# Transposes of q, k and x moved from the PE to DMA, in a kernel whose instruction order is planned beforehand

## The chip, the cores and the metric

One core of a Trainium2 chip. The time is device microseconds (us) of one execution, the median of several runs; lower is better. A ratio is the mean time of one kernel's fast runs over the mean of the other's fast runs of the same rounds on the same chip, so it is not quite the ratio of the medians quoted next to it. The runs were made in several calls on different chips; where times from two calls are compared, the ratios to the kernel before are what counts. All runs were in the fast state but one of e8 and one of e17; their ratios leave it out.

The engines are called PE (matrix products), DVE, ACT and POOL (here exponentials, masks, casts and copies) and SP (issues the DMAs here). Operands lie in one memory of the core, SBUF. In this kernel the PE writes its results to another, PSUM, and DVE or ACT copies them from there: 24 copies of 0.55 us for the transposed q and k of batches 1 to 3. The granted clock is the share of its full speed at which the PE was allowed to run.

## The reference

Attention with a window of 128 keys and 4 sink keys, over 4 batches, 8 heads, 768 positions and head dimension 64, followed by a two-layer network with a sigmoid-type gate on the 3072 tokens:

```python
scores = scale * q @ k.T                       # per batch and head
keep = (key < 4) | ((0 <= pos_q - pos_k) & (pos_q - pos_k < 128))
a = softmax(where(keep, scores, -1e9)) ; attn = a @ v
x = attn.transpose(0, 2, 1, 3).reshape(3072, 512)
h = x @ w_in                                   # 512 x 2048
out = (h * sigmoid(1.702 * h)) @ w_out         # 2048 x 512
```

## The kernel before

Work is cut into 32 units of one head pair and 384 positions (`kk`), 16 load groups of two units (`m`), and 8 slabs of the network (`n`), each fed by four units. The prediction calls a unit a head pair. Nothing is ordered by hand: every operation is declared with an engine, a duration that the author believes, and its predecessors, and a small scheduler plays the machine once when the kernel is built. It then emits the instructions in the order in which they started in that play. **Each engine executes its own instructions in that fixed order**, and SP's queue of DMA issues is one of the "engines". A wrong duration therefore cannot make the result wrong, but it puts instructions in an order that the chip then has to wait through.

```python
class Plan:
    LAG = {"PE": 0.2, "SP": 1.6}           # what a follower on another engine waits beyond the duration
    def order(self, idle):
        ...                                # pick, engine by engine, what can start first
            free[eng] = start + o["dur"]
            end[n] = free[eng] + self.LAG.get(eng, 0.12)
        ...
        return sorted(out, key=lambda x: x[:2])
```

Loads go over SP, three DMAs of 128 KB for each of q, k and v of a group in batches 1 to 3. POOL casts them to fp16; POOL also applies most of the masks, in the same fixed order:

```python
dur = 1.25 if b == 0 else 1.75
load(f"Lq{m}", dur, ...) ; load(f"Lk{m}", dur, ...) ; load(f"Lv{m}", 1.8, ...)
...
op(f"Cq{m}", "POOL", ...) ; op(f"Ck{m}", "POOL", ...)      # casts
op(f"MZ{kk}_{t}", "POOL", 0.4, ...)                        # masks of unit kk
op(f"V{kk}", "PE", ..., after=masked + ...)                # attention times v, waits for the masks
```

The parts that the change replaces, for batches 1 to 3:

```python
def t_mm():                                    # q and k of one unit: 6 transposes into PSUM
    for t in range(2):
        for i in range(NB):
            nc.tensor.transpose(tp[:, t, i], qk[:, t, i], ident16)
op(f"T{kk}", "PE", 0.36, t_mm, ...) ; op(f"Tc{kk}", "DVE", 0.65, ...)      # and a copy to SBUF
...
def x_mm():                                    # x of one unit: 3 transposes into PSUM
    for i in range(NB):
        nc.tensor.transpose(xt[:, i], T[f"xn{kk}"][:, i], ident16)
op(f"X{kk}", "PE", 0.2, x_mm, ...) ; op(f"Xc{kk}", "DVE", 0.37, x_copy, ...)
```

The softmax here doesn't subtract the row's maximum and nothing guards it: scores larger than these inputs give would overflow.

Of the kernel before, what the change touches and what calls it, by code (L numbers as in the profile page):

```python
# [14 lines left out]
P = 128  # L15
D = 64
SLAB = 384
NB = SLAB // P
# [19 lines left out]
class Plan:  # L38
# [14 lines left out]
    def op(self, name, eng, dur, emit, after=(), opens=(), uses=(), rank=0.0, at=0.0, starts=()):  # L53


        assert name not in self.ops
        self.ops[name] = dict(
            name=name, eng=eng, dur=dur, emit=emit, after=list(after), starts=list(starts),
            opens=list(opens), rank=rank, at=at,
        )  # L60
        for t in set(uses) | {t for _, t in opens}:
            self.users.setdefault(t, set()).add(name)
# [74 lines left out]
def kernel(  # L137
# [11 lines left out]
    nc = tc.nc  # L149
    Bsz, H, S, Dh = q.shape  # L150
# [6 lines left out]
    NHP = H // 2  # L157
    NU = 2 * NHP
# [7 lines left out]

    slots = dict(
        ps=8,
        qk32=4, v32=4, w32=3, qk16=4, v65=6, qkT=8, AT0=2, AT1=2, xnat=2, th=3, gT=2, xT=4, osb=2,
    )  # L170
    const = ctx.enter_context(tc.tile_pool(name="const", bufs=1))
    sb = ctx.enter_context(tc.tile_pool(name="sb", bufs=1))
# [2 lines left out]
    T = {}  # L175

    def new(name, shape, dt=FP16):
        tag, i = plan.slot_of[name]
        pool = psp if tag == "ps" else sb
        T[name] = pool.tile(list(shape), dt, tag=f"{tag}{i}", bufs=1, name=name)  # L180
        return T[name]
# [3 lines left out]
    ident16 = const.tile([P, P], FP16, name="ident16")  # L185
# [8 lines left out]
    op = plan.op  # L194
# [61 lines left out]
    def add_casts(m: int, eq: str, ek: str, ev: str):  # L256
        b, g, hp = where(2 * m)
        dur = {"DVE": 0.56, "ACT": 0.83, "POOL": 0.85}

        def qk(t, eng):  # L260
            if t == 0:
                new(f"qk16_{m}", (P, 2, NB, 4, D))
            dst, src = T[f"qk16_{m}"][:, t], T[f"qk32_{m}"][:, t]
            if b == 0:
                ENG[eng](  # L265
                    dst.rearrange("p i h d -> p h i d"),
                    src.rearrange("p (h i d) -> p h i d", i=NB, d=D),
                )
            else:
                ENG[eng](dst.rearrange("p i h d -> p (i h d)"), src)  # L270

        op(f"Cq{m}", eq, dur[eq], lambda: qk(0, eq), after=[f"Lq{m}"],
           opens=[("qk16", f"qk16_{m}")], uses=[f"qk32_{m}"], rank=2 * m)
        op(f"Ck{m}", ek, dur[ek], lambda: qk(1, ek), after=[f"Lk{m}", f"Cq{m}"],
           uses=[f"qk16_{m}", f"qk32_{m}"], rank=2 * m)

        def cv():
            v65 = new(f"v65_{m}", (P, NB, 4, D1))
            nc.gpsimd.memset(v65[:, :, :, D:D1], 1.0)
            ENG[ev](v65[:, :, :, 0:D], T[f"v32_{m}"])  # L280

        op(f"Cv{m}", ev, dur[ev] + 0.1, cv, after=[f"Lv{m}"], opens=[("v65", f"v65_{m}")],
           uses=[f"v32_{m}"], rank=2 * m + 0.5)
        if g == 0:
            def sink(c):
                pool(
                    vs[c][32 * c : 32 * c + n_sink, H * b + 2 * hp : H * b + 2 * hp + 4],
                    T[f"v65_{m}"][0:n_sink, 0],
                )

            for c in range(3):
                op(f"K{m}_{c}", "POOL", 0.44, lambda c=c: sink(c), after=[f"Cv{m}"],
                   uses=[f"v65_{m}"], rank=2 * m + (0.6 if c == 0 else 5))


    def qkT(kk):
        return T[f"qkT{kk}"]

    def half(kk: int):
        m, j = divmod(kk, 2)  # L300
        return T[f"qk16_{m}"][:, :, :, 2 * j : 2 * j + 2]
# [5 lines left out]
    def add_attention(kk: int, at: float):  # L307
        b, g, hp = where(kk)
        m = kk // 2
# [1 line left out]
        r = kk  # L311
        at_ = f"AT{kk}"
        prev = kk - NHP if g else kk
        qts = [f"qkT{kk}"] + ([f"qkT{prev}"] if g else [])

        if early:

            def t_mm(t):
                qk = half(kk)
                if t == 0:  # L320
                    new(f"qkT{kk}", (P, 2, NB, P))
                tp = new(f"tp{kk}_{t}", (P, SLAB), FP32)
                for i in range(NB):
                    nc.tensor.matmul(  # L324
                        tp, qk[:, t, i], spread[:, i], start=(i == 0), stop=(i == NB - 1)
                    )

            def t_copy(t, eng):
                eng(qkT(kk)[:, t].rearrange("d i s -> d (i s)"), T[f"tp{kk}_{t}"])

            for t, eng in enumerate(("DVE", "ACT")):
                op(f"T{kk}_{t}", "PE", 0.5, lambda t=t: t_mm(t),
                   after=[f"C{'qk'[t]}{m}", "spread"] + ([f"SA{kk - 1}"] if kk else []), opens=[("ps", f"tp{kk}_{t}")] + ([] if t else [("qkT", f"qkT{kk}")]),
                   uses=[f"qk16_{m}"], rank=r)
                op(f"Tc{kk}_{t}", eng, (0.56, 0.48)[t],
                   lambda t=t, eng=eng: t_copy(t, ENG[eng]),
                   after=[f"T{kk}_{t}"] + ([f"Tc{kk}_0"] if t else []),
                   uses=[f"tp{kk}_{t}", f"qkT{kk}"], rank=r)
            ready = [f"Tc{kk}_0", f"Tc{kk}_1"]
        else:  # L340
            def t_mm():
                qk = half(kk)
                tp = new(f"tp{kk}", (P, 2, NB, P))
                for t in range(2):
                    for i in range(NB):
                        nc.tensor.transpose(tp[:, t, i], qk[:, t, i], ident16)  # L346

            op(f"T{kk}", "PE", 0.36, t_mm, after=[f"Cq{m}", f"Ck{m}", f"SA{kk - 1}"],
               opens=[("ps", f"tp{kk}"), ("qkT", f"qkT{kk}")], uses=[f"qk16_{m}"], rank=r, at=at)
            op(f"Tc{kk}", "DVE", 0.65,  # L350
               lambda: dve(new(f"qkT{kk}", (P, 2, NB, P)), T[f"tp{kk}"]),  # L351
               after=[f"T{kk}"], uses=[f"tp{kk}", f"qkT{kk}"], rank=r)
            ready = [f"Tc{kk}"]

        def mm(dst, h, key, i0, ni):
            nc.tensor.matmul(  # L356
# [10 lines left out]
        def s_z():  # L367
            Z = [new(f"Z{kk}_{h}", (P, 512), FP32) for h in range(2)]
            pk = qkT(prev)
            for h in range(2):  # L370
                mm(Z[h][:, 0:P], h, qkT(kk)[:, 1, 2], 2, 1)
            for h in range(2):
                if g:
                    mm(Z[h][:, P : 2 * P], h, pk[:, 1, 2], 0, 1)
                else:
                    mm(Z[h][:, P : 2 * P], h, pk[:, 1, 0], 2, 1)
            if g:
                for c in range(4):
                    for h in range(2):
                        mm(  # L380
                            Z[h][bass.ts(c, 32), 2 * P : 3 * P], h,
                            pk.rearrange("d t i s -> d t (i s)")[:, 1, 0:32], min(c, 2), 1,
                        )

        def e_a(h):
# [15 lines left out]
        op(f"SZ{kk}", "PE", (0.2, 0.36)[g], s_z, after=[f"SA{kk}"],  # L401
           opens=[("ps", f"Z{kk}_{h}") for h in range(2)], uses=qts, rank=r)
        for h in range(2):
            op(f"EA{kk}_{h}", "ACT", 0.5, lambda h=h: e_a(h),
               after=[f"SA{kk}"] + ([f"EA{kk}_0"] if h else []),
               opens=[] if h else [(f"AT{g}", at_)], uses=[f"A{kk}_{h}", at_], rank=r)
        for h in range(2):
            op(f"EZ{kk}_{h}", "ACT", (0.3, 0.4)[g], lambda h=h: e_z(h),
               after=[f"SZ{kk}", f"EA{kk}_1"], uses=[f"Z{kk}_{h}", at_], rank=r)

        def m_a():
# [13 lines left out]

        masked = []
        if g == 0 or early:
            op(f"MA{kk}", "DVE", 0.7, m_a, after=[f"EA{kk}_0", f"EA{kk}_1", "masks"], uses=[at_], rank=r)
            masked.append(f"MA{kk}")
        else:  # L430
            for t, sgn in ((0, 1), (1, -1)):
                op(f"MA{kk}_{t}", "POOL", 0.64,
                   lambda t=t, sgn=sgn: select(0, 8, 2, t, sgn), after=[f"EA{kk}_0", f"EA{kk}_1"],
                   uses=[at_], rank=r)
                masked.append(f"MA{kk}_{t}")
        for t, sgn in ((0, 1), (1, -1))[: 1 + g]:
            op(f"MZ{kk}_{t}", "POOL", 0.4,
               lambda t=t, sgn=sgn: select(8, 8 + 2 * SZ[g], SZ[g], t, sgn),
               after=[f"EZ{kk}_0", f"EZ{kk}_1"], uses=[at_], rank=r)
            masked.append(f"MZ{kk}_{t}")  # L440
# [47 lines left out]
        def x_copy():  # L488
# [1 line left out]
                new(f"xT{n}", (P, NHP, SLAB))  # L490
            dve(T[f"xT{n}"][:, hp].rearrange("p (i s) -> p i s", s=P), T[f"xt{kk}"])  # L491

        op(f"X{kk}", "PE", 0.2, x_mm, after=[f"N{kk}", "ident"], opens=[("ps", f"xt{kk}")],
           uses=[f"xn{kk}"], rank=r)
        op(f"Xc{kk}", "DVE", 0.37, x_copy, after=[f"X{kk}"] + ([f"Xc{kk - 1}"] if hp else []),
           opens=[] if hp else [("xT", f"xT{n}")], uses=[f"xt{kk}", f"xT{n}"], rank=r)


    def add_f(n: int, F: int):
# [17 lines left out]
        def f_mul():  # L517
# [8 lines left out]
           after=[f"Xc{4 * n + 3}", f"W{F // 4}"] + ([f"F{n}_{F - 1}"] if F else []),  # L526
           opens=[("ps", f"hT{nm}")] + ([] if F else [("gT", f"gT{n}")]),
           uses=[f"xT{n}"], rank=rank)
        op(f"H{nm}", "ACT", 0.42, f_tanh, after=[f"F{nm}"], opens=[("th", f"th{nm}")],
           uses=[f"hT{nm}"], rank=rank)  # L530
        op(f"G{nm}", "DVE", 0.555, f_mul, after=[f"H{nm}"],
           uses=[f"hT{nm}", f"th{nm}", f"gT{n}"], rank=rank)
# [150 lines left out]
```

## Time and profile before

| | before |
|---|---|
| time, median (three runs at first, a fourth with the change) | 249.29 us, 249.89 us |
| span of the profiled run | 247.7 us |
| PE busy | 231.7 us (94%) |
| PE without work between 50 and 160 us | 110.0 - 106.7 = 3.3 us |
| SP issues the last load of q, k or v until | 114.2 us |
| POOL's casts wait for loads of q, k and v | 13.7 us |

The stretch from 50 to 160 us, with the columns that the prediction explains, and the PE's wait for POOL's masks (us in total, times, longest):

```profile
50.00:160.00 110.00, 106.68 (x1080) 63.38 (x1081) 68.10 (x150) 64.83 (x149) 57.55 (x108) 1.00 0.65 144
...
PE av L461 <- POOL AT L420: 2.5, 3, 1.9
```

The PE is the engine to fill. Its busy time is that of overlapping matmul records, so what it says well is where the PE has nothing at all to do. POOL's waits matter only as far as they reach the PE.

### The profile page before, as it was taken

The page shows a single profiled execution, that of the slowest core. Times are in us where ns is not written, and L with a number is a line of the kernel's source. Part 1 is how long each engine was busy: PE and PEld are TensorE (multiplying, and loading weights), DVE is VectorE, ACT ScalarE, POOL GpSimd, SP SyncE. Part 2 cuts the span into 40 slices and gives each one's busy share as a digit, 9 for nine tenths or more (in the row PEclk, how much of TensorE's full clock was granted, in tenths as well). Part 3 has the DMA queues.
Part 4 walks back from the last instruction along what each step waited for, and adds up shares of the span by engine and source line. Part 5 has one row for each costly group of instructions (what it writes and reads, how often), then busy time and mean ns, then how long its engine had stood idle before and what let it go on. Part 6 is the DMA issues. An engine that isn't in the chain of part 4 may idle for free.

```text
span 247.7 us, 5387 instructions
## 1 busy us (share of the span) xinstructions
PE 231.7 (94%) x2065; PEld 132.8 (54%) x2065; DVE 135.8 (55%) x282; ACT 132.0 (53%) x291; POOL 102.1 (41%) x171
## 2 busy tenths in 40 slices
PE   0996999989999699999999999999999999999993
PEld 0453566556555465565555665556654554564441
DVE  6376589678646563378724787348731680382000
ACT  2472788367547472487644784458741661472111
POOL 7688487687467786643267400015330000000000
PEclk9998999999999999999999999999999999999999
DMA  7999999899997999996011100120002101201112
GB/s 186 294 371 282 329 356 315 199 230 216 237 242 184 231 202 237 225 241 146 3 45 42 45 3 0 51 79 4 0 10 77 42 3 44 83 0 45 75 53 86
DMA packets 75723, 34.14 MB, mean 138 GB/s; under 512 B 64177, under 2 KB 68657, under 8 KB 75697
## 3 DMA queue, kind: packets, MB, share of 16 engines
q1 hardware_dynamic: 75552, 33.76, 52.7%
q8 instruction: 16, 0.26, 0.5%
q14 instruction: 11, 0.08, 0.1%
q10 hardware_dynamic: 144, 0.03, 0.1%
HBM read 27.49 MB, written 6.29 MB: 136 GB/s over the span
## 4 chain that ended last, share of the span: by engine, by line
PE 72%; DMA 7%; POOL 7%; SPq 7%; ACT 2%; DVE 2%; issue 2%; ACTq 0%; POOLq 0%
PE o L542 30%; PE hT L507 25%; SPq L220 6%; DMA v<-in_v_dram 6%; PE av L461 4%; PE A L356 3%; PE tp L324 3%; PE tp L346 2%; POOL AT L420 2%; PE Z L356 2%; DMA qk<-in_k_dram 2%; PE xt L484 2%; DVE vs L587 1%; POOL w_in L253 1%; POOL v L280 1%
## 5 line engine op out<-in xcount | busy, mean ns | idle before, releaser
L507 PE MATMUL hT<-xT,w_in 128*128 128x384 f16 x512 | 92.6, 328 | 0.2 <-ACT AT L388 0.2
L542 PE MATMUL o<-w_out,gT 128*128 128x512 f16 x384 | 89.2, 379 | 0.0
L520 DVE SCALAR_TENSOR_TENSOR gT<-th,hT 128x384 f16<-128x384 f16 x128 | 67.1, 548 | 35.0 <-ACT th L513 31.6
L513 ACT ACTIVATE th<-hT 128x384 f16<-128x384 f32 x128 | 60.9, 504 | 30.1 <-PE hT L507 27.8
L507 PEld LDWEIGHTS <-w_in 128*128 128x128 f16 x512 | 47.6, 98 | 29.4 <-issue 1.4
L420 POOL TENSOR_SCALAR_AFFINE_SELECT AT<-AT 128x256 f16<-128x256 f16 (+1 forms) x72 | 35.1, 513 | 56.1 <-ACT AT L394 23.2
L542 PEld LDWEIGHTS <-gT 128*128 128x128 f16 x384 | 35.7, 98 | 38.1 <-issue 0.2
L388 ACT ACTIVATE AT<-A 128x512 f16<-128x512 f32 x64 | 34.7, 595 | 22.1 <-PE A L356 22.1
L560 ACT ACTIVATE osb<-o 128x512 f32<-128x512 f32 x23 | 13.8, 601 | 45.0 <-PE o L542 37.6
L394 ACT ACTIVATE AT<-Z 128x256 f16<-128x256 f32 (+1 forms) x64 | 24.8, 452 | 0.0
L270 POOL CAST qk<-qk 128x768 f16<-128x768 f32 x24 | 19.4, 824 | 9.4 <-PE tp L346 3.8
L461 PEld LDWEIGHTS <-AT 128*128 128x128 f16 x480 | 18.4, 97 | 8.9 <-POOL AT L420 3.7
L414 DVE TENSOR_TENSOR AT<-AT,masks 128x1024 f16<-128x1024 f16 x20 | 16.5, 824 | 12.0 <-ACT AT L388 11.9
L461 PE MATMUL av<-v,AT 128*128 128x65 f16 x352 | 19.2, 193 | 3.5 <-POOL AT L420 2.5
L470 DVE TENSOR_TENSOR xn<-av,rcp 128x384 f16<-128x384 f32 x32 | 17.8, 557 | 1.1
L356 PEld LDWEIGHTS <-qkT 64*128 64x128 f16 (+1 forms) x384 | 11.5, 93 | 11.9 <-DVE xT L491 3.0
L324 PE MATMUL tp<-spread,qk 128*128 128x384 f16 x48 | 11.5, 369 | 6.5 <-DVE qk L265 6.0
L351 DVE COPY qkT<-tp 128x768 f16<-128x768 f16 x24 | 13.2, 552 | 6.9 <-PE tp L346 6.8
L280 POOL CAST v<-v 128x768 f16<-128x768 f32 x16 | 13.2, 826 | 8.6 <-DMA v<-in_v_dram 8.4
L469 DVE RECIPROCAL rcp<-av 128x6 f32<-128x6 f32 x32 | 6.2, 194 | 17.9 <-PE av L461 17.4
L491 DVE COPY xT<-xt 128x384 f16<-128x384 f16 x32 | 11.3, 354 | 7.2 <-PE xt L484 5.9
L461 PE MATMUL av<-vs,AT 128*128 128x65 f16 x128 | 14.9, 193 | 0.0
(30 smaller groups left out, 131.4 us busy)
## 6 DMA issues: line engine op xcount, KB each, us to landing
v<-in_v_dram SPq DMA_DIRECT2D x48, 128.0 KB, 3.6
out_dram<-osb SPq DMA_DIRECT2D x23, 256.0 KB, 2.0
qk<-in_q_dram SPq DMA_DIRECT2D x36, 128.0 KB, 3.5
qk<-in_k_dram SPq DMA_DIRECT2D x36, 128.0 KB, 3.7
w<-in_moe_w_in_dram SPq DMA_DIRECT2D x4, 1024.0 KB, 7.1
w<-in_moe_w_out_dram SPq DMA_DIRECT2D x4, 1024.0 KB, 8.5
qk<-in_q_dram SPq DMA_DIRECT2D x4, 384.0 KB, 5.7
qk<-in_k_dram SPq DMA_DIRECT2D x4, 384.0 KB, 6.1
```

The source lines that it names most:

```text
L270: ENG[eng](dst.rearrange("p i h d -> p (i h d)"), src)
L324: nc.tensor.matmul(tp, qk[:, t, i], spread[:, i], start=(i == 0), stop=(i == NB - 1))
L356: nc.tensor.matmul(dst.rearrange("p (t s) -> p t s", s=P), key[hd[h]], qkT(kk)[hd[h], 0, i0 : i0 + ni], start=True, stop=True,)
L388: nc.scalar.activation(out=T[at_][:, 4 * h : 4 * h + 4].rearrange("p a s -> p (a s)"), in_=T[f"A{kk}_{h}"], func=AF.Exp, scale=scale,)
L394: nc.scalar.activation(out=T[at_][:, 8 + SZ[g] * h : 8 + SZ[g] * (h + 1)].rearrange("p a s -> p (a s)"), in_=T[f"Z{kk}_{h}"][:, 0 : SZ[g] ...
L420: nc.gpsimd.affine_select(out=ap, in_=ap, pattern=[[0, ap.shape[1]], [sgn, P]], compare_op=ALU.is_ge if sgn > 0 else ALU.is_gt, fill=0.0, ...
L461: nc.tensor.matmul(av[:, i, h], lhsT, rhs, start=(n == 0), stop=(n == len(terms) - 1))
L470: nc.vector.tensor_tensor(out=xn, in0=av[:, :, :, 0:D], in1=rcp.to_broadcast((P, NB, 2, D)), op=ALU.mult)
L507: nc.tensor.matmul(hT, w_in16[:, c, bass.ts(F, P)], T[f"xT{n}"][:, c], start=(c == 0), stop=(c == NHP - 1),)
L513: nc.scalar.activation(out=new(f"th{nm}", (P, SLAB)), in_=T[f"hT{nm}"], func=AF.Tanh, scale=0.851)
L520: nc.vector.scalar_tensor_tensor(out=T[f"gT{n}"][:, F], in0=T[f"th{nm}"], scalar=1.0, in1=T[f"hT{nm}"], op0=ALU.add, op1=ALU.mult,)
L542: nc.tensor.matmul(T[f"o{nm}"], T[f"gT{n}"][:, F, bass.ts(t, P)], w_out16[:, F], start=(F == 0), stop=(F == NF - 1),)
```

## The change

The intent is to take 216 transposes off the full PE, and their PSUM copies off DVE, and to let DMA do them from SBUF to SBUF: q and k of a group in one transpose of 384 KB, x of a unit in one of 96 KB. All are issued by SP, between the loads and the stores. Some durations of ACT, DVE and POOL are corrected on the way, and the numbers of buffers are changed.

```diff
-        qk32=4, v32=4, w32=3, qk16=4, v65=6, qkT=8, AT0=2, AT1=2, xnat=2, th=3, gT=2, xT=4, osb=2,
+        qk32=3, v32=4, w32=3, qk16=3, v65=6, qkT=8, qkTm=5, AT0=2, AT1=2, xnat=4, th=3, gT=2, xT=4, osb=2,
...
+        if b > 0:
+            op(f"T{m}", "SP", 1.4,
+               lambda: nc.sync.dma_start_transpose(
+                   new(f"qkTm{m}", (P, 2, NB, 2, P)).rearrange("d t i j s -> d (t i j) s"),
+                   T[f"qk16_{m}"].rearrange("s t i h d -> s (t i h d)"),
+               ),
+               after=[f"Cq{m}", f"Ck{m}"], opens=[("qkTm", f"qkTm{m}")], uses=[f"qk16_{m}"],
+               rank=-1)
...                                            # in place of the PE's T and DVE's Tc
+            ready = [f"T{m}"]
...
-            op(f"EA{kk}_{h}", "ACT", 0.5, ...
+            op(f"EA{kk}_{h}", "ACT", 0.55, ...   # likewise EZ, MA, MZ, H: 10 to 20% longer
...
+        else:                                  # batches 1 to 3, in place of the PE's X and DVE's Xc
+            def x_dma():
+                ...
+                nc.sync.dma_start_transpose(
+                    T[f"xT{n}"][:, hp].rearrange("p (i s) -> p i s", s=P),
+                    T[f"xn{kk}"].rearrange("s i h d -> s (i h d)"),
+                )
+            op(f"Xc{kk}", "SP", 0.5, x_dma, after=[f"N{kk}"] + ([f"Xc{kk - 1}"] if hp else []), ..., rank=-2)
```

## The prediction

> **What bounds the kernel now.** I read the page first (busy shares, slices, chain of work), then the stretches of 10 us, then the PE's timeline in one of them, then who waits for whom on the queue of SP. The first lines of the page:
>
> ```profile
> span 247.7 us, 5387 instructions
> PE 231.7 (94%) x2065; PEld 132.8 (54%) x2065; DVE 135.8 (55%) x282; ACT 132.0 (53%) x291; POOL 102.1 (41%) x171
> DMA  7999999899997999996011100120002101201112
> PE 72%; DMA 7%; POOL 7%; SPq 7%; ACT 2%; DVE 2%; issue 2%; ACTq 0%; POOLq 0%
> ```
>
> The PE is busy 94% and makes 72% of the chain that ended last. DVE and ACT are at half. The DMA row is full for its first 18 slices (about 111 us) and nearly empty afterwards. So there are two parts: up to about 115 us the loads (mostly 256-byte rows) keep the DMA engines full and take a share of the chain; after it only the PE counts. The stretches show it:
>
> ```profile
> 40.00:50.00 10.00, 9.69 (x90) 5.77 (x88) 7.66 (x16) 4.96 (x12) 6.84 (x7) 1.00 0.88 243
> 50.00:60.00 10.00, 9.49 (x87) 5.90 (x88) 7.96 (x17) 7.56 (x19) 8.11 (x15) 1.00 1.16 225
> 80.00:90.00 10.00, 8.09 (x86) 5.23 (x85) 6.12 (x14) 6.45 (x16) 7.46 (x14) 1.00 1.13 218
> 110.00:120.00 10.00, 10.00 (x96) 6.27 (x95) 8.87 (x20) 7.19 (x18) 2.53 (x4) 1.00 0.59 130
> 140.00:150.00 10.00, 10.00 (x109) 6.71 (x107) 8.86 (x21) 7.84 (x19) 0.99 (x3) 1.00 0.01 2
> ```
>
> Columns: stretch, length, busy us of PE, weight load, DVE, ACT, POOL, then the granted clock, the DMA share, GB/s. From 110 us on the PE has no free time; between 40 and 90 us it has a little (8.09 of 10 at worst), and there the loads are the reason: POOL waits for them.
>
> ```profile
> POOL v L280 <- DMA v<-in_v_dram: 8.4, 10, 1.7
> POOL qk L270 <- DMA qk<-in_k_dram: 3.4, 4, 1.0
> POOL qk L270 <- DMA qk<-in_q_dram: 1.9, 3, 0.8
> ```
>
> That is 13.7 us of POOL waiting for loads. POOL casts and masks in one fixed order, so a late load holds up the masks behind it, and the PE behind those.
>
> **What a transpose costs the PE.** "Busy" counts pipelined matmuls at full length, so I take the distance from the first transpose to the start of what follows on the PE:
>
> ```profile
> 134.86 0.50 PE L346 MATMUL tp<-ident,qk 128*128 128x128 f16 x6
> 135.19 0.23 PE L461 MATMUL av<-v,AT 128*128 128x65 f16 x2
> ...
> 137.11 0.34 PE L484 MATMUL xt<-ident,xn 128*128 128x128 f16 x3
> 137.28 3.41 PE L507 MATMUL hT<-xT,w_in 128*128 128x384 f16 x20
> ```
>
> Six q/k transposes hold the PE for 135.19 - 134.86 = 0.33 us, three x transposes for 0.17 us, about 56 ns each, although one is recorded with some 220 ns.
>
> **What the Trainium skill says.** "TensorE: Matmul & The Clock Gate", Part 4: PE-mode transpose, gives about 275 ns for a transpose in a kernel and 390 ns alone, with a DVE copy after it. The records here are 219 ns, the distance 56 ns: the page's number is a latency, and only the distance counts on a full PE. "VectorE: DVE Perf Modes", The three transpose paths, gives 1309 ns for 128x128 by DMA, against 390 on the PE. The kernel before has no DMA transpose, so its trace cannot confirm this. "DMA: Bandwidth & Descriptors", Latency and other measured facts, gives 261 GB/s for DMA transposes with a non-contiguous middle dimension; not in this trace either, but the strided loads here run at 218 to 243 GB/s. "Advanced Engine Details and Errata", DGE: Hardware vs Software, calls transpose efficiency worse for the hardware generator, which is the one used from SP. No number stands with that, and it is my main doubt.
>
> **What the change removes.** Batch 0 keeps the PE path (24 of 32 head pairs change). PE: 24 x 0.33 = 7.9 us for q and k, 24 x 0.17 = 4.1 us for x: 12.0 us, nearly all on the path, as these lie between 49 and 187 us where the PE is full. DVE: 24 copies of 0.552 us and 24 of 0.354 us, 13.2 + 8.5 = 21.7 us. DVE has a busy share of 55%, so that pays nothing by itself; it only shortens delays. PSUM also loses two kinds of tile, which relieves the eight slots.
>
> **What it adds.** On SP, 12 transposes of 128x1536 fp16 (384 KB each) and 24 of 128x384 (96 KB): 4.7 + 2.4 = 7.1 MB beside 34.14 MB. With the page's 261 GB/s this is an estimate of 27 us of full DMA, 1.5 us for a large one and 0.4 us for a small one. They come mostly in the stretch in which DMA is already full. The order of the built program shows all 36 in the one in-order queue between loads and stores: the first large one stands right behind three loads of the next group and waits for casts on POOL, and everything behind it waits too. SP's issues are not free: three copies took about 1.6 us there, 0.53 us each.
>
> **Does the load stream still fit?** The issues of the 12 load groups of batches 1 to 3 run from 37.3 to 114.2 us, 6.4 us a group (pure issue 9 x 0.53 = 4.8, the rest waiting). A group serves two head pairs, and the q/k transposes of 24 head pairs now run from 49.4 to 178.4 us: 129 / 23 x 2 = 11.2 us a group, about 10.5 us with the PE time saved. Adding 1.5 for the large one and 2 x 0.5 for the small ones (issue-bound like a copy) makes 8.9 us a group, 107 us in all, ending near 144 us instead of 114 us. So it fits, with some 1.6 us a group to spare. But the scheduler puts POOL's casts where it expects the loads, so not all of that is usable slack.
>
> **What is given back.** The first q/k transpose has no slack: the cast ended at about 50.5 us and scores started about 1 us later; now a DMA comes between, and loads landed in 3.5 us here while the queue was full, against some 1 us for PE plus copy. I count 3 us of PE standing still for the first two groups and 1 us for the first slab's last x, of which 1 us is hidden by the free PE time that is there anyway: net 3 us. The three-slot buffers for q/k (four before) hold the early loads a little more; I count zero. Later, the SP order has groups further and further ahead of their use, so nothing there.
>
> **Sum.** 249.3 - 12.0 + 3 = 240.3 us. I say 240.
>
> **The rivals.** (1) A transpose holds SP or the DMA engines far longer than a copy of its size. At 5 us for a large and 1.3 for a small one (an assumption, the DMA 3.4 times slower than the estimate) a group takes 6.4 + 5 + 2.6 = 14 us, 3.5 us more than the PE needs: 12 x 3.5 = 42 us late, of which the last quarter is hidden by the 55 us of pure matmuls at the end: 255 to 280 us. For: the page's "worse", 1309 ns for a single block, one in-order queue. Against: the author's scheduler counts 1.4 and 0.5 us for the two, beside engine durations which have been moved to what the profile shows (0.55 for the Exp, 0.48 for the tanh), so these were probably measured too. (2) Landing time and cast waits take over at every group, because the PE's order is fixed: 1 us for each of 12 groups cancels the gain, 248 to 250 us. For: POOL's 13.7 us of waiting for loads already, and a DMA row that is full. Against: the transposes of later groups are issued several head pairs ahead. (3) The stream is smooth and even the start is hidden: 249.3 - 12 = 237 us, perhaps 235 with the PSUM slots freed. For: the PE idles little today.
>
> **Range and chances.** The middle case and (3) give 235 to 244 us, and I give them 0.58 (244.3 us is 2% below). Case (2), 244 to 254 us: 0.18. Case (1): 0.24, with a long tail, so the range is lopsided: 233 to 266 us.
>
> **What would show each step.** Right: no transposes after the first batch on the PE, PE busy lower by about 12 records' worth of distance (busy falls by more, some 15 us), DVE lower by 22 us; large transposes landing within about 5 us and SP held under 2 us by each; last load issued at 135 to 150 us; a full PE from there. The PE's stretch from 50 to 70 us should show 3 to 4 us idle released by the transposing DMA. Wrong: SP held 3 us or more by each large transpose, POOL waits on loads well above 14 us, PE holes past 100 us whose releaser is a DMA. The prediction fails altogether if the slices show DMA full to 180 us, for then the transposes set the pace.

## The result, and the profile after

257.74 us (256.86 to 257.92) against 249.89 us: ratio 1.0314, 95% interval 1.0251 to 1.0377. The change is 3% slower. The prediction said 240 us, faster. The page of the changed kernel, the lines that answer to the first ones of the prediction:

```profile
span 255.1 us, 4977 instructions
PE 224.8 (88%) x1852; PEld 120.7 (47%) x1852; DVE 116.1 (46%) x234; ACT 132.8 (52%) x291; POOL 101.9 (40%) x171
DMA  7999999899989888899998989222012101200122
PE 50%; SPq 17%; DMA 13%; POOL 4%; issue 3%; ACT 3%; DVE 2%; POOLq 0%; ACTq 0%; DVEq 0%
```

The PE did lose instructions (2065 to 1852) and busy time, and DVE lost 19.7 us. But the PE's share of the span fell from 94% to 88%, and of the chain that ended last from 72% to 50%. SP's queue and the DMAs have taken its place, 7 + 7% before and 17 + 13% after. DMA is full for 25 slices (of 6.4 us, so 160 us) in place of 18. The stretches, same columns as in the prediction:

```profile
50.00:60.00 10.00, 8.63 (x71) 4.79 (x70) 6.15 (x12) 7.37 (x17) 5.85 (x13) 1.00 1.16 204
100.00:110.00 10.00, 6.98 (x69) 3.58 (x67) 2.20 (x5) 2.83 (x6) 5.81 (x12) 1.00 0.85 192
140.00:150.00 10.00, 7.35 (x62) 3.88 (x61) 3.29 (x7) 4.51 (x10) 6.68 (x14) 0.83 0.94 216
170.00:180.00 10.00, 10.00 (x79) 5.45 (x77) 6.10 (x13) 7.08 (x18) 0.81 (x2) 1.00 0.22 64
```

The PE has holes until 160 us: over 50 to 160 us it is without work for 110.0 - 91.5 = 18.5 us, where it was 3.3 us. From 170 us on it is full again. Who waits for whom (us in total, times, longest):

```profile
POOL qk L270 <- DMA qk<-in_k_dram: 23.7, 11, 4.0
POOL v L280 <- DMA v<-in_v_dram: 16.8, 13, 2.5
POOL qk L270 <- DMA qk<-in_q_dram: 16.0, 8, 4.4
PE av L463 <- POOL AT L422: 13.4, 8, 2.7
PE A L358 <- DMA qkTm<-qk: 3.4, 2, 2.0
PE hT L521 <- DMA xT<-xn: 2.1, 1, 2.1
```

POOL's casts now wait 56.5 us for loads (13.7 before). The PE waits 13.4 us for POOL's masks (2.5 before). It waits only 5.5 us for the transposes themselves. One such hole in the timeline, start and duration first, the wait in brackets:

```profile
98.95 1.18 SPq L504 DMA_TRANSPOSE xT<-xn  x1
...
100.24 1.45 SPq L285 DMA_TRANSPOSE qkTm<-qk  x1
101.74 2.01 SPq L220 DMA_DIRECT2D qk<-in_k_dram  x3
...
105.56 0.38 PE L463 MATMUL av<-v,AT 128*128 128x65 f16 x7
...
106.47 0.82 POOL L270 CAST qk<-qk 128x768 f16<-128x768 f32 x1 [2.65 <-DMA qk<-in_k_dram]
107.25 0.40 POOL L422 TENSOR_SCALAR_AFFINE_SELECT AT<-AT 128x256 f16<-128x256 f16 x1
...
107.70 0.20 PE L463 MATMUL av<-v,AT 128*128 128x65 f16 x1 [1.77 <-POOL AT L422]
```

SP issues a small and a large transpose and only then the loads of k. POOL comes to the cast of that k and stands for 2.65 us. Behind the cast in its order is a mask, of a unit that has nothing to do with that load; and the PE, in the middle of the products of that unit, stands for 1.77 us until the mask is done.

The sum: the PE's work shrinks by the 12.0 us of the prediction, its holes between 50 and 160 us grow by 18.5 - 3.3 = 15.2 us, and the clock record of the trace has two stretches of 3.4 us at half clock instead of one, which costs 1.7 us. That is +4.9 us, against +7.4 us in the spans. The remaining 2.5 us I did not place. The page shows on which side they lie: over the whole span the PE's busy time fell by 231.7 - 224.8 = 6.9 us only, not by 12.0, and the slower clock explains 1.7 of these 5.1 us.

What the transposes took, first of SP (ns: least, median, most), then from issue to landing (us, median):

```profile
L285 SPq DMA_TRANSPOSE qkTm<-qk x12: 1273/1505/3065, 50.3 to 156.6; - x12
L504 SPq DMA_TRANSPOSE xT<-xn x24: 1178/1179/2183, 61.9 to 205.7; - x24
...
xT<-xn SPq DMA_TRANSPOSE x24, 2.7
...
qkTm<-qk SPq DMA_TRANSPOSE x12, 3.9
```

The large one holds SP for 1.5 us, as counted. The small one, a quarter of the bytes, holds it for 1.18 us, where the kernel's scheduler counts 0.5 us.

### The profile page after: what moved, and what is told of

The parts are those of the page before. It is cut to its first block, busy times and chain, and to the rows that moved or that the text cites. A ratio compares the mean times of both kernels' runs of the same rounds, so it can differ in the third digit from the quotient of the medians.

```text
span 255.1 us, 4977 instructions
## 1 busy us (share of the span) xinstructions
PE 224.8 (88%) x1852; PEld 120.7 (47%) x1852; DVE 116.1 (46%) x234; ACT 132.8 (52%) x291; POOL 101.9 (40%) x171
## 4 chain that ended last, share of the span: by engine, by line
PE 50%; SPq 17%; DMA 13%; POOL 4%; issue 3%; ACT 3%; DVE 2%; POOLq 0%; ACTq 0%; DVEq 0%
PE o L556 24%; PE hT L521 18%; SPq L220 12%; DMA v<-in_v_dram 5%; DMA qk<-in_k_dram 4%; PE av L463 3%; SPq L285 2%; PE A L358 2%; DMA qkTm<-qk 2%; POOL AT L422 2%; PE Z L358 1%; ACT AT L390 1%; SPq L504 1%; PE tp L338 1%; DMA qk<-in_q_dram 1%
## 5 line engine op out<-in xcount | busy, mean ns | idle before, releaser
L556 PE MATMUL o<-w_out,gT 128*128 128x512 f16 x384 | 87.3, 379 | 0.0
L534 DVE SCALAR_TENSOR_TENSOR gT<-th,hT 128x384 f16<-128x384 f16 x128 | 66.3, 550 | 42.2 <-ACT th L527 38.9
L527 ACT ACTIVATE th<-hT 128x384 f16<-128x384 f32 x128 | 59.9, 501 | 28.3 <-PE hT L521 22.9
L521 PEld LDWEIGHTS <-w_in 128*128 128x128 f16 x512 | 48.4, 99 | 35.4 <-issue 5.2
L270 POOL CAST qk<-qk 128x768 f16<-128x768 f32 x24 | 20.3, 845 | 39.8 <-DMA qk<-in_k_dram 23.7
L463 PE MATMUL av<-v,AT 128*128 128x65 f16 x352 | 19.7, 193 | 14.0 <-POOL AT L422 13.4
L416 DVE TENSOR_TENSOR AT<-AT,masks 128x1024 f16<-128x1024 f16 x20 | 15.9, 794 | 18.2 <-ACT AT L390 18.2
L358 PEld LDWEIGHTS <-qkTm 64*128 64x128 f16 (+1 forms) x288 | 8.6, 95 | 13.7 <-issue 7.8
L463 PE MATMUL av<-vs,AT 128*128 128x65 f16 x128 | 14.9, 193 | 0.0
L358 PE MATMUL A<-qkTm 64*128 64x256 f16 x96 | 9.8, 285 | 3.4 <-DMA qkTm<-qk 3.4
L295 POOL COPY vs<-v 4x260 f16<-4x260 f16 x24 | 9.7, 404 | 1.3
```

Source lines behind the costliest of these rows:

```text
L270: ENG[eng](dst.rearrange("p i h d -> p (i h d)"), src)
L358: nc.tensor.matmul(dst.rearrange("p (t s) -> p t s", s=P), key[hd[h]], qkT(kk)[hd[h], 0, i0 : i0 + ni], start=True, stop=True,)
L463: nc.tensor.matmul(av[:, i, h], lhsT, rhs, start=(n == 0), stop=(n == len(terms) - 1))
L521: nc.tensor.matmul(hT, w_in16[:, c, bass.ts(F, P)], T[f"xT{n}"][:, c], start=(c == 0), stop=(c == NHP - 1),)
L527: nc.scalar.activation(out=new(f"th{nm}", (P, SLAB)), in_=T[f"hT{nm}"], func=AF.Tanh, scale=0.851)
L534: nc.vector.scalar_tensor_tensor(out=T[f"gT{n}"][:, F], in0=T[f"th{nm}"], scalar=1.0, in1=T[f"hT{nm}"], op0=ALU.add, op1=ALU.mult,)
```

## The experiments

Theories at the start. **Q**: SP's queue is overloaded, loads come late, and with them POOL's casts and the masks behind them. **B**: the bytes of the transposes crowd the DMA engines. **O**: SP has time enough, but the order of POOL, PE and SP was planned with wrong SP times. Later runs separate Q from O.

All results in one table; ratio is to the kernel before in the same rounds. "Holes" is PE without work between 50 and 160 us, "last load" is when SP had issued the last load of q, k or v, both read from the profiled run. "Planned" is when the scheduler counted that this would happen, from a replay of the plan in each run's kernel.py; "late" is the difference. The plan starts its first load about 1 us earlier than the chip, in every run.

| run | time us (before there) | ratio, 95% interval | holes us | last load us | planned us | late us |
|---|---|---|---|---|---|---|
| the kernel before | 249.89 | | 3.3 | 114.2 | 104.5 | 9.7 |
| the change | 257.74 (249.89) | 1.031, 1.025 to 1.038 | 18.5 | 155.2 | 127.2 | 28.0 |
| e1_qk_only | 250.72 (248.71) | 1.005, 1.000 to 1.010 | 9.1 | 133.4 | 117.2 | 16.2 |
| e2_x_only | 250.96 (248.71) | 1.007, 1.003 to 1.011 | 7.6 | 126.5 | 111.3 | 15.2 |
| e3_replan | 244.57 (248.71) | 0.982, 0.977 to 0.988 | 8.4 | 161.1 | 143.9 | 17.2 |
| e6_tiny_copies | 264.29 (248.71) | 1.061, 1.058 to 1.064 | 13.5 | 151.4 | 127.1 | 24.3 |
| e4_v_on_act | 271.97 (249.20) | 1.092, 1.087 to 1.096 | 25.1 | 138.6 | 100.0 | 38.6 |
| e5_x_pairs | 255.55 (249.20) | 1.025, 1.019 to 1.030 | 14.9 | 149.7 | 125.8 | 23.9 |
| e7_no_transposes | 249.80 (249.20) | 1.003, 0.999 to 1.006 | 2.9 | 116.6 | 110.8 | 5.8 |
| e8_before_lag3 | 251.52 (249.20) | 1.007, 1.000 to 1.014 | 2.3 | 112.4 | 104.5 | 7.9 |
| e9_replan_loads | 235.91 (248.40) | 0.948, 0.944 to 0.952 | 0.7 | 167.6 | 160.9 | 6.7 |
| e12_pairs_replan_loads | 234.83 (248.40) | 0.943, 0.940 to 0.947 | 1.6 | 150.2 | 143.2 | 7.0 |
| e13_qk_replan_loads | 238.22 (248.40) | 0.959, 0.956 to 0.962 | 0.0 | 139.2 | 134.1 | 5.1 |
| e15_tiny_replan | 247.37 (248.40) | 0.995, 0.992 to 0.997 | 0.0 | 165.5 | 160.3 | 5.2 |
| e14_before_replan_loads | 245.93 (248.44) | 0.991, 0.987 to 0.994 | 0.0 | 115.9 | 112.9 | 3.0 |
| e16_told_transposes | 245.20 (248.44) | 0.989, 0.985 to 0.992 | 8.8 | 164.5 | 148.1 | 16.4 |
| e17_told_loads | 252.77 (248.44) | 1.016, 1.011 to 1.022 | 12.1 | 160.5 | 136.6 | 23.9 |

All gave correct results. The numbering has gaps; no e10 or e11 is on record.

Over these 17 kernels the holes follow the lateness (from 3 us late and no hole to 38.6 us late and 25.1 us of holes, correlation 0.99) and not the time of the last load itself (0.23). A correlation alone does not say what causes what, for a hole can also delay the SP queue; the runs with unchanged instructions, below, do.

**e1_qk_only.** The x transposes go back to the PE.

```diff
-        if early:
+        if True:
             op(f"X{kk}", "PE", 0.2, x_mm, ...
```

> q and k transposed by DMA as in the change, x again by the PE and DVE. Theory Q (the in-order SP queue is what is overloaded: 1.5 us for each large and 1.18 us for each small transpose, so that loads, POOL's casts and the masks behind them come late): 24 x 1.18 = 28 us of SP go away, about 20 of them before the last load; the last load is issued near 135 us instead of 155, PE's waits for POOL masks fall from 13.4 us to under 6, and the time is 241 to 247 us. Theory B (the bytes of the transposes crowd the DMA engines): two thirds of the bytes stay, so two thirds of the holes stay: 253 to 259 us.

250.72 us. The last load (133.4 us) and the PE's wait for masks (5.8 us) came as Q said, the time did not: 4 us above its range. Removing the small transposes gains 7 us on the change, yet the large ones alone still leave 9.1 us of holes: with 16.2 us, the last load is still far behind this run's own plan. B's 253 to 259 us was missed too.

**e2_x_only.** The converse: T and its DVE copy back on the PE path, x by DMA.

```diff
-            op(f"T{m}", "SP", 1.4, ...dma_start_transpose...)
+            op(f"T{kk}", "PE", 0.36, t_mm, ...) ; op(f"Tc{kk}", "DVE", 0.65, ...)
```

> x transposed by DMA as in the change, q and k again by the PE and DVE. Theory Q: the scheduler counts 0.5 us for a small transpose and SP takes 1.18, so about 15 us too little up to the last load; the PE gains 4 us and loses some 6 to 10 in holes: 251 to 256 us. Theory B: one third of the bytes, holes of 4 to 5 us against 4 us gained: 249 to 252 us. If the failing part were only the large transposes, this would be faster than before: 246 us.

250.96 us, at the edge of both ranges, so it does not choose. It does say that neither kind of transpose is the culprit alone: each kind costs as much as it saves.

**e3_replan.** Not one instruction is changed, only what the scheduler believes.

```diff
-    LAG = {"PE": 0.2, "SP": 1.6}
+    LAG = {"PE": 0.2, "SP": 3.0}
-            op(f"T{m}", "SP", 1.4,
+            op(f"T{m}", "SP", 1.6,
-            op(f"Xc{kk}", "SP", 0.5, x_dma, ...
+            op(f"Xc{kk}", "SP", 1.25, x_dma, ...
```

> The same instructions as the change; only the scheduler is told what the trace shows (1.6 us for a large, 1.25 us for a small transpose, 3.0 us to landing for a DMA), so the fixed orders of POOL, PE and SP change. Theory O (order: SP is full but fast enough, the casts merely stand too early in POOL's order): holes fall from some 18 us between 50 and 160 us to under 6, 238 to 246 us. Theory Q in its strict form, and theory B (not enough SP or DMA time whatever the order): 253 to 258 us.

244.57 us: 1.8% faster than the kernel before, where the change was 3.1% slower (some 12 us between them), although SP finishes the loads even later (161.1 us). The holes fell to 8.4 us, a little more than O said. Q in its strict form and B cannot explain this.

**e6_tiny_copies.** The kernel before, plus 84 copies of 512 bytes that nobody reads, in the places of the transposes. (The text on record says "same waits"; that was inexact. They stand in the same places of the plan, but on the chip they wait for no cast and no x, so only their issue counts.)

```diff
+            op(f"D{m}", "SP", 1.4, lambda: tiny(3), after=[f"Cq{m}", f"Ck{m}"], rank=-1)
+            op(f"Dx{kk}", "SP", 0.5, lambda: tiny(2), after=[f"N{kk}"], rank=-2)
```

> The kernel before, with its PE transposes, and in the places of the DMA transposes 3 and 2 copies of 512 bytes on SP that nobody reads (0.5 us of issue each, so 1.5 and 1.0 us, as the transposes took; same waits, no bytes to speak of). Theory Q: the load stream slows as in the change, the last load is issued near 150 us and PE holes appear: 256 to 266 us. Theory B: 249 to 252 us, no holes.

264.29 us. Next to no bytes, and the damage is all there: 15.6 us more than before. The stretch from 50 to 160 us:

```profile
50.00:160.00 110.00, 96.50 (x939) 56.11 (x937) 59.94 (x128) 57.76 (x131) 54.85 (x104) 0.97 0.59 138
```

The DMA share is 0.59, so the DMA engines have room, and the PE lacks work for 13.5 us. B as the main cause falls. All of these holes are of the kind seen in the change, the PE waiting for a mask on POOL:

```profile
PE av L471 <- POOL AT L430: 13.5, 8, 3.6
```

Of the 15.6 us, 10.2 are holes that the kernel before did not have in this stretch; two more stretches of 3.4 us at half clock are worth another 3.4 us.

**e4_v_on_act.** The loads of v move to ACT's queue. (The plan also counts 3.0 us of landing for the loads of v, which the cut does not show.)

```diff
+            op(f"Lv{m}", "ACT", 1.6,
+               lambda: blocks(new(f"v32_{m}", (P, NB, 4, D), FP32), v, nc.scalar),
+               opens=[("v32", f"v32_{m}")], starts=[f"Lk{m}"], rank=2 * m)
```

> The change, but the 36 loads of v of batches 1 to 3 are issued from ACT's queue (same bytes, 36 x 0.53 = 19 us less for SP, as much more for ACT, busy 52%). Theory Q/O (SP's queue runs later than the scheduler expects): SP is ahead again, waits of POOL for loads and of PE for masks fall by more than half, 239 to 246 us. Theory B (bytes): no better than 254 us. A miss through ACT being held up at its own queue would show as PE waiting for Exp.

271.97 us, the slowest of all, through the miss that was named. From its timeline:

```profile
66.27 3.64 ACTq L220 DMA_DIRECT2D v<-in_v_dram  x3
...
69.96 0.66 ACT L401 ACTIVATE AT<-Z 128x256 f16<-128x256 f32 x2 [4.49 <-DMA v<-in_v_dram]
70.39 2.72 PE L526 MATMUL hT<-xT,w_in 128*128 128x384 f16 x8 [4.33 <-ACT AT L401]
```

ACT stands at its own DMA issue for 4.49 us before an Exp, and the PE behind it for 4.33 us. SP was relieved (last load 138.6 us), but a queue that belongs to a computing engine passes its waits to the computation. The granted clock of this run was 0.949 on average, the lowest of all; the trace has 27.3 us at half clock (one stretch of 6.8 and two of 10.2 us), beside its 25.1 us of holes.

**e5_x_pairs.** x of two units in one transpose: 12 of 192 KB for 24 of 96 KB. (With three of the doubled x buffers it did not fit in SBUF; it has two, the same memory as the four single ones.)

```diff
-            op(f"Xc{kk}", "SP", 0.5, x_dma, after=[f"N{kk}"] + ..., opens=[] if hp else ...)
+            if hp % 2:
+                op(f"Xc{kk}", "SP", 0.8, x_dma, after=[f"N{kk}", f"N{kk - 1}"] + ..., opens=[] if hp > 1 else ...)
```

> The change with x transposed for two head pairs at once: 12 transposes of 192 KB in place of 24 of 96 KB, the same bytes. If SP pays per instruction (a large one took 1.27 us at least, a small one 1.18, so about 1.2 whatever the size), 12 x 1.2 = 14 us of SP go, some 9 of them before the last load: 248 to 253 us. If SP or the DMA engines pay by the byte: 256 to 259 us, as the change.

255.55 us, between the two ranges. The mechanism was right:

```profile
L506 SPq DMA_TRANSPOSE xT<-xn x12: 1212/1220/2585, 64.7 to 201.6; - x12
```

Twice the bytes take 1.22 us of SP in place of 1.18, so SP pays nearly the same per instruction. But the time gained only some 2 us. The last load came 5.5 us earlier, not 9, and the order still did not expect what it met.

**e7_no_transposes** keeps the change's buffers and durations, with all transposes on the PE (e1 and e2 together).

> The change without any DMA transpose: only its other edits (three buffers in place of four for q and k in both types, four for the normalized x, longer durations in the scheduler for Exp, tanh and masks). If these edits cost nothing, 248 to 251 us, as before. If the smaller buffers were what delays the loads, 254 us or more.

249.80 us: the side edits cost nothing measurable.

**e8_before_lag3** is the kernel before with `LAG` for SP at 3.0.

> The kernel before with nothing changed but the scheduler's landing time of a DMA, 3.0 in place of 1.6 us. A control for the replanned change: if the better order alone explains its gain, this one gains too (246 us or less). I expect little, 247 to 251 us, as the loads of the kernel before already run close to what its scheduler counts.

251.52 us, no gain: a longer landing alone does not make e3's gain. (One of its four executions was in the slow state; the median of the other three is 251.10 us.)

**e9_replan_loads.** As e3, with the loads told as well, which measured about 0.65 us for each DMA of 128 KB in the load stream, waits included (three in 2.0 us):

```diff
-    LAG = {"PE": 0.2, "SP": 1.6}
+    LAG = {"PE": 0.2, "SP": 3.2}
-        dur = 1.25 if b == 0 else 1.75                  # v likewise: 1.8 to 2.0
+        dur = 1.25 if b == 0 else 2.0
-            op(f"T{m}", "SP", 1.4,
+            op(f"T{m}", "SP", 1.7,
-            op(f"Xc{kk}", "SP", 0.5, x_dma, ...
+            op(f"Xc{kk}", "SP", 1.35, x_dma, ...
```

> As the replanned change, with the loads told too: three loads 2.0 us in place of 1.75, large transposes 1.7, small ones 1.35, landing 3.2 us. In the replanned change the last load was still issued 19 us later than the scheduler counted (161 against 142 us), and 8.4 us of PE holes were left between 50 and 160 us. Theory O: with the rest of the error gone the holes fall below 5 us, 238 to 243 us. If SP's time itself is the limit now: 244 to 250 us, as SP is told to be full to 159 us.

235.91 us, 5.2% faster than before and better than the range of either theory. The same stretch of the change, and then of this run:

```profile
50.00:160.00 110.00, 91.50 (x791) 48.91 (x789) 46.08 (x96) 58.38 (x130) 54.63 (x105) 0.97 0.96 196
```

```profile
50.00:160.00 110.00, 109.35 (x979) 59.05 (x977) 56.78 (x117) 71.17 (x158) 55.50 (x104) 1.00 0.91 192
```

The same bytes, nearly the same DMA share (0.91 against 0.96) and GB/s (192 against 196). The last load is issued 12 us later than in the change. Yet the PE's holes go from 18.5 to 0.7 us. Its waits:

```profile
PE av L463 <- POOL AT L422: 0.4, 1, 0.4
...
PE A L358 <- DMA qkTm<-qk: 0.2, 1, 0.2
```

What differs is the order, of POOL, PE and SP together. POOL around load group 9 (units 18 and 19), from the replay of the plans, numbers being places in POOL's list of operations; in the change:

```
72 cast qk16_9 (q)
73 to 76 masks of unit 14
78, 79 casts qk16_9 (k) and v of group 9
80 to 83 masks of unit 15
```

and in e9:

```
68 to 71 masks of unit 14
72 to 75 masks of unit 15
79, 80 casts qk16_9 (q and k)
```

In the change a cast for units 18 and 19 stands ahead of the masks of units 14 and 15; that is the place where it would start if SP were as fast as believed. In e9 the urgent masks go first. The place alone does no harm: in e14 below, where the last load is 3.0 us late and no hole is left, even more masks stand behind the k cast of a later unit (masks of earlier units behind the k casts of groups 4 to 15: 123, against 99 in the change and 26 in e9). It does harm when the load comes much later than the plan counted. That POOL's order alone, without those of PE and SP, makes the gain was not tested.

**e12_pairs_replan_loads** puts e5's pairs and e9's times together (large 1.7, double x 1.4, three loads 2.0, landing 3.2).

> x transposed for two head pairs at once, with the scheduler told the measured times (large 1.7, double x 1.4, three loads 2.0, landing 3.2 us). Needs 12 fewer issues. Theory O and Q together: 237 to 242 us, the best of the study. If only the order counts, as the replanned change without pairs.

234.83 us, below the range, the best of the study. Its interval overlaps with that of e9, so that the pairs are worth something is not shown. With the order right, fewer issues on SP buy little.

**e13_qk_replan_loads**: e1 with large 1.9, three loads 2.0, landing 3.2.

> Only q and k by DMA, scheduler told the measured times (large 1.9, three loads 2.0, landing 3.2 us). The PE keeps 4.1 us for the x transposes. Theory O: the time of the unplanned one (250.7) falls by its holes: 241 to 246 us.

238.22 us, below O's range as well. The x transposes by DMA are worth 238.2 - 235.9 = 2.3 us more, where 4.1 us of PE work were counted.

**e15_tiny_replan**: e6 with its copies told as 1.9 and 1.3 us, three loads 2.0, landing 3.2.

> The kernel before with the 84 tiny copies that took it from 249 to 264 us, but now the scheduler is told what they take (1.9 us for three, 1.3 us for two, three loads 2.0, landing 3.2 us). Theory O: the same SP work in an order that expects it costs little, 249 to 255 us. If SP's occupancy itself costs the time whatever the order: 261 to 266 us.

247.37 us, 17 us less than e6 with the same instructions, and not above the kernel before. The stretch:

```profile
50.00:160.00 110.00, 110.00 (x1099) 64.36 (x1098) 69.53 (x152) 67.86 (x153) 55.02 (x107) 1.00 0.58 137
```

No hole at all, with SP issuing loads until 165.5 us. SP's occupancy as such costs next to nothing here; not having planned for it costs some 15 us. The fair base is e14 below, the kernel before with the same told loads: against it the copies cost 247.37 - 245.93 = 1.4 us (ratios 0.995 and 0.991, their intervals overlap). e6 and e15 are the cleanest pair of the study.

By now 12 runs had been made; three more settled what each told time is worth.

**e14_before_replan_loads**: the kernel before with three loads 2.0 and landing 3.2.

> The kernel before, with the scheduler told the loads' measured times (three loads 2.0 us, landing 3.2 us), no DMA transpose. Control: if the better order alone explains the 236 us of the replanned change, this one comes near 240 us. If the transposes are what pays, it stays at 245 to 250 us.

245.93 us, in the second range: better told loads are worth 1% to the kernel before. So the worth of the DMA transposes, with equally good orders on both sides, is about 245.9 - 235.9 = 10 us (two calls on two chips, each beside a kernel before of 248.4 us).

**e16_told_transposes**: the change, large 1.7, small 1.35, nothing else.

> The change, with the scheduler told only the transposes (1.7 and 1.35 us); loads 1.75 us for three and landing 1.6 us as in the change. If the small transposes counted at 0.5 us were the error that matters, most of the gain is here: 236 to 243 us. If it is the loads or the landing: 248 to 255 us.

**e17_told_loads**: the change, three loads 2.0 and landing 3.2, nothing else.

> The change, with the scheduler told only the loads (three in 2.0 us) and the landing (3.2 us); transposes 1.4 and 0.5 us as in the change. The counterpart: 248 to 255 us if the transposes' error matters most, 236 to 243 us if the loads' does. If both land near 244 to 248 us, it is the sum of the errors on SP that counts and not a single one.

245.20 and 252.77 us, from 257.74 (whose kernel before ran 1.5 us slower than the one here; one of e17's four executions was slow, the median of the others is 252.19 us). e16 misses its first range by 2 us, e17 lies in its own, and both help. By the ratios (1.031 for the change; 0.989, 1.016 and 0.948 for e16, e17 and e9), telling the transposes gains 4.3%, or some 11 us, telling the loads and the landing 1.5%, or some 4 us, both together 8.4%, or some 21 us. The transposes' error was the larger, but neither alone removes the holes: with e16 the PE still had 8.8 us of them, with its last load 16.4 us late.

## Why the prediction was wrong

**What the transposes cost the PE: about right.** 12.0 us were counted. With orders of like quality on both sides (e14 against e9) the DMA transposes gain 10 us.

**The load stream's arithmetic: nearly right.** 8.9 us a group and an end near 144 us were expected; it was 117 / 12 = 9.8 us (37.9 to 155.2 us) and 155 us. The mis-sized term is the small transpose, "issue-bound like a copy", 0.5 us: it held SP for 1.18 us. By the SP timeline, 14 of the 24 fell between 37.9 and 155.2 us and took 19.1 us there, waits included, which is 1.6 us a group where 1.0 was counted; the rest of the difference is more output stores (9 for 6) and gaps. The large ones at 1.5 us were met. 9.8 us is still under the 10.5 us that the PE needs, so by the prediction's own argument it fitted.

**The step that failed is what followed from "So it fits".** The text said that "not all of that is usable slack", because POOL's casts are placed where the scheduler expects the loads, and then counted nothing for it. In place of the average rate, what decides is whether each load lands about when the fixed order expects it. In the change the last load came 28.0 us after the planned time. e9 shows it from one side: the stream ends still later, at 167.6 us, but only 6.7 us after its plan, with 0.7 us of holes. e6 and e15 show it from the other: the same SP work costs some 15 us or next to nothing. What is "given back" was put at 3 us net, for the first transposes. That term was about right (the PE waited 3.4 us for the first large transposes, between 50 and 70 us), but the holes grew by 15.2 us in all. Read from 48 to 160 us, the PE's waits for POOL's masks grew by 11.5 - 2.5 = 9.0 us, and 5.5 us of waits for transposes, these 3.4 us among them, came on top.

**"So these were probably measured too": wrong.** The other corrected durations are within some 15% of the trace (0.55 us counted and 0.60 measured for one Exp, 0.34 and 0.40 for another, 0.48 and 0.50 for the tanh); 0.5 us for the small transpose was not half of what the chip took. That inference was the argument against rival (1), and so for the 0.58.

**Rivals.** Rival (1) has the time in its range (255 to 280 us) for the wrong reason: no transpose held SP for 5 us (3.1 us at most in the change), and neither SP nor DMA had to be faster. Rival (2), landing and cast waits, is the mechanism, but it was sized at 12 us of waits, where the holes grew by 15.2 us, and given a small chance because "the transposes of later groups are issued several head pairs ahead". That is true of the transposes, and the PE waited little for them; it is not true of the casts and masks on POOL. Rival (3) is what e9 and e12 reach: 236 and 235 us.

**The signs named beforehand.** Of the signs of being right, the 3 to 4 us idle between 50 and 70 us, DVE's fall (19.7 us, 22 said) and the landing of the large transposes (3.9 us) came about. The last load was 5 us past its range, and PE busy fell by 6.9 us where "some 15 us" was said ("about 12 records' worth of distance" must mean 12 us of distance). Of the signs of being wrong, "POOL waits on loads well above 14 us" came true (56.5 us), and so did holes past 100 us, but not by the releaser that was named: 9.7 us there are waits for a POOL mask (behind a late cast, as in the hole shown), and none is put down to a DMA directly. "SP held 3 us or more by each large transpose" did not come true (median 1.5 us).

**What stays open.** 2.5 us of the change's loss are not placed. The told times are a little longer than what SP was held for (1.35 us for 1.18, 1.7 for 1.5), so it is not separated whether a plan needs the true times or a margin. Why e1, with nearly right large transposes, ran 16.2 us behind its plan was not taken apart; in e13, with the told times, it is 5.1 us behind, and no hole is left.

## What to carry to other kernels

When engines run in a fixed order that was planned with assumed durations, a change that adds work to one queue must be measured, written back into the plan and planned again before it is judged: here the very same instructions are 3% slower or 5% faster than before. Read a stall not only by its releaser but by what stands ahead of the releaser in its engine's order: a mask that waits behind someone else's cast. And ask of a queue not only whether its average rate suffices, but who is placed behind each of its deliveries. A quick check, in these 17 kernels: when the last load came at most 7 us later than planned, at most 2.9 us of holes were left.

## What the Trainium skill lacked or had wrong

- "DMA: Bandwidth & Descriptors" names no figure for how long a DMA transpose between SBUF tiles holds the issuing queue of this chip (it has cycle counts of "previous generations", beside those of another chip; no run here gives cycles). Here it is nearly independent of the size, at the least 1.18 us for 96 KB, 1.21 us for 192 KB and 1.27 us for 384 KB, against 0.53 us for a plain copy in a row of three.
- "VectorE: DVE Perf Modes", The three transpose paths, gives 1309 ns for one 128x128 block by DMA and nothing for several. Multiplying it by the blocks would mislead: three blocks landed 2.7 us after issue, six 2.9 us (e5) and twelve 3.9 us (medians), so a further block is worth about (3.9 - 2.7) / 9 = 0.13 us, an estimate. A single block was not run.
- "Advanced Engine Details and Errata", DGE: Hardware vs Software, calls transposes from the hardware generator worse, without a number. No run here transposes by the software generator, so the comparison is not tested. It did not hinder: the change with a fitting order (e9) was 5.2% faster than the kernel before.
- "TensorE: Matmul & The Clock Gate", Part 4, gives 275 ns for a transpose in a kernel; in a row on a full PE they stand 56 ns apart here. 216 of them make 12.0 us, and removing them was worth about 10 us (e14 against e9).
- No page was found to say that a load issued from ACT can hold up ACT's computing: 4.49 us ahead of one Exp in e4, for 36 loads moved from SP, and 272 us in place of 258.
